# A hand-fused attention and gating kernel on one core: the same pieces of work in another order on every queue

## The chip, the core and the metric

The kernel runs on one core of one Trainium2 chip. A core has five instruction queues that run side by side: TensorE (PE, matmuls), VectorE (DVE), ScalarE (ACT), GpSimd (POOL) and SyncE (SP, which here only issues DMAs). Each takes its instructions strictly in the order in which they were written, and waits for what an instruction needs. The metric is the device time of one execution in microseconds; smaller is better.

## What is computed

Attention in which a query sees only the keys of its own cluster, for 4 batches, 8 heads, 768 positions and 64 features, and then a gated MLP on the joined heads:

```python
q_assign = np.argmax(np.einsum('bhsd,hcd->bhsc', q_n, c_n), axis=-1)   # 16 clusters a head
k_assign = np.argmax(np.einsum('bhsd,hcd->bhsc', k_n, c_n), axis=-1)
mask = q_assign[:, :, :, None] == k_assign[:, :, None, :]
scores = np.where(mask, scale * np.matmul(q, k.transpose(0, 1, 3, 2)), -1e9)
attn = np.exp(scores - np.max(scores, axis=-1, keepdims=True))
attn = attn / (np.sum(attn, axis=-1, keepdims=True) + 1e-09)
x = np.matmul(attn, v)                 # heads joined: 4 x 768 x 512
h = np.maximum(x @ w_in, 0.0)          # 512 -> 1024
u, v = h[..., :512], h[..., 512:]      # v is layer-normalised over its 512
v_s = np.einsum('ts,bsd->btd', w_spatial, v_n) + b_spatial[None, :, None]
out = (u * v_s) @ w_out                # 512 -> 512
```

## The kernel before

The work falls into pieces: a piece is a handful of instructions on one engine, or one DMA issue. The functions `prep`, `shifts`, `attend` and `mlp` (with `v_tile`, `u_tile`, `s_tile`, `p_tile`) only describe them to a plan: which engine, which pieces must be over first, which buffers are taken. The loop at L1156 goes through 4 batches of 4 pairs of heads and describes the preparation of the next pair, the attention of this pair, and after each batch its MLP. `Plan.run` then writes the program. What stands where on each queue is not decided by a rule: it is read from a table, one list of numbers for each engine, in which a number is the count of a piece among those of its engine:

```python
            own = [o for o in self.ops if o.eng == e]
            queue[e] = [own[int(k)] for k in ORDER.get(e, "").split()][::-1]
```

There are 847 pieces on PE, 730 on ACT, 967 on DVE, 294 on POOL and 330 on SP. Pieces of attention, of the preparation of later heads and of the MLP of the batch before stand mixed on each queue, so that PE has other work while a score waits for its exponential.

The pieces that come up below, by their lines:

- Head of the program: 76 filler matmuls on a constant tile (L560) run before and between the first pieces of PE; L586 transposes the centroids.
- Preparation of a pair: L695 casts the features to their high half (ACT), L704 makes the low half, L710 copies it (DVE), L741 to L743 are the cluster logits (PE), L760 to L764 the argmax on DVE, L772 and L773 the one-hot form (ACT), L788 brings its rows in beside the features and L789 copies features on (lo<-hq), both as DMAs that SP issues. L815 and L816 sum the values, L826 and L828 write their means. L859 (PE) and L866 (DVE) find row maxima of the scores, L878 to L882 turn them into shifts.
- Attention in row form, for the heads that a list names: scores L920 and L922 (PE), maximum and scale L925 to L927 (DVE), exponential L928 and its high half L930 (ACT), low half L931 (POOL), a DMA that transposes both (L936, p<-pt, issued by SP), values L940 (PE).
- Attention in column form, for the others: scores L956 and L958 (PE), exponential L962 and high half L964 (ACT), low half L965 (POOL), values L970 (PE). No DMA stands between.
- The attention's output is divided and split in L989 to L994 and transposed in L996.
- MLP: L1015 (matmuls for v and for the output), L1037 to L1049 the layer norm on DVE, L1050 (ACT) and L1051 (POOL) its halves vn, L1075 (matmuls for u and for the spatial mix), L1108 to L1113 the gate, L1138 and L1139 the output.

The buffers on which pieces wait for one another: 2 score buffers (sc) and 4 accumulators (acc) in PSUM; 6 tiles each of p in 32 bits (p32) and of its halves (pt); 3 of hq and lo; 2 of v32, 4 of u32.

Of the kernel before, what the change touches and what calls it, by code (L numbers as in the profile page):

```python
# [137 lines left out]
8 20 40 72 18 27 46 62 11 9 59 35 6 16 14 5 76 4 34 54 37 33 7 78 57 31 81 49 41 63 51 12 84 80 79 24 60 19 29 83 73 36 0 85 87 38 17 91 92 93 82 90 88 3 42 58 86 22 89 39 106 48 101 95 77  # L138
32 94 47 1 25 103 100 107 26 99 52 56 98 126 50 96 128 10 102 130 132 150 2 97 134 116 108 136 104 127 105 129 109 138 140 110 131 113 142 111 114 117 144 115 133 123 112 146 118 148 119 125
135 121 137 120 139 141 124 70 143 64 65 122 194 152 170 155 172 158 145 147 174 160 176 161 178 154 156 159 180 21 167 168 149 66 157 13 169 171 163 45 153 173 182 53 162 55 184 166 71 75  # L140
186 67 188 175 165 177 190 179 181 192 183 15 164 185 74 214 196 216 238 198 187 218 151 189 191 193 220 222 202 23 205 224 204 68 69 203 199 200 226 201 228 197 215 230 213 211 232 217 212
234 219 221 206 195 223 209 236 208 227 207 229 225 210 258 231 240 260 249 262 248 264 243 247 241 336 266 245 233 253 235 268 254 252 237 270 244 246 242 255 251 272 250 274 256 259 261 30
257 276 278 263 280 239 271 265 267 269 347 349 371 338 351 273 275 43 353 28 277 340 344 279 281 44 61 339 345 355 357 348 343 350 341 352 359 361 337 363 342 346 354 365 373 380 379 356
378 367 374 358 360 369 282 362 364 283 375 382 376 384 381 284 377 386 388 406 366 285 390 392 372 368 394 370 396 286 287 288 289 398 383 294 385 387 400 407 389 295 391 408 402 412 393
292 404 414 293 290 291 441 299 300 304 415 305 413 416 309 411 417 310 419 395 397 409 399 410 421 443 444 423 446 451 401 425 296 449 450 297 427 445 403 298 429 405 306 431 311 307 433
308 312 418 435 313 420 422 424 301 302 437 439 303 426 322 323 447 452 428 448 430 324 454 432 325 456 434 458 530 436 460 453 438 462 455 464 440 326 466 457 314 315 468 316 470 459 442
317 472 474 461 463 320 318 321 319 541 465 543 532 467 538 537 535 469 545 547 533 471 565 549 473 536 551 540 553 475 327 555 534 328 542 544 539 546 557 329 548 559 550 330 561 331 563
476 477 478 552 479 554 531 590 566 568 556 558 570 572 560 332 574 562 480 564 576 578 481 580 333 567 582 482 483 569 584 334 335 586 588 484 571 573 579 575 591 581 577 486 593 485 595
615 488 487 597 583 489 585 599 493 601 587 498 494 589 603 499 592 605 594 503 607 596 609 504 598 611 490 600 613 491 616 602 604 492 500 606 618 620 501 502 495 622 608 496 610 624 612
614 626 505 497 628 630 617 506 619 507 632 694 621 634 623 516 625 636 517 638 627 521 522 695 697 518 629 519 631 699 520 523 701 633 635 719 524 703 637 525 705 639 707 510 696 709 508  # L150
698 509 700 711 511 713 702 640 715 641 717 704 642 706 512 643 720 722 652 708 644 653 724 710 645 712 726 744 714 728 646 647 730 716 718 513 732 514 734 515 721 648 723 649 736 725 657
738 658 727 740 650 742 729 731 651 733 745 662 663 747 667 735 749 668 526 751 737 739 527 741 753 743 755 654 655 757 759 659 746 656 748 761 660 750 763 661 765 752 664 767 754 528 756
769 665 758 760 771 666 529 773 762 775 669 764 766 777 670 779 680 781 770 768 681 783 671 785 772 774 685 787 789 776 686 778 791 682 683 780 687 688 689 782 784 786 684 674 788 790 675
792 672 676 673 677 678 679 793 794 795 796 797 798 799 805 800 803 801 806 804 802 810 815 690 691 816 692 811 693 820 821 817 822 818 812 813 823 807 808 809 814 824 819 833 838 834 839
835 836 840 827 837 829 841 842 825 826 828 830 831 832 845 843 844 846
""",
    "ACT": """
0 1 23 24 2 35 36 25 28 27 26 29 31 30 32 44 46 45 47 7 50 33 51 34 38 40 37 39 8 48 49 85 86 59 61 60 63 65 62 64 41 43 42 67 66 69 68 72 88 87 74 70 73 76 78 75 77 53 54 55 80 123 124 52
# [1053 lines left out]
```

## Time and profile before

| | us |
|---|---|
| runs of the kernel before, median of 3 (lowest, highest) | 615.07 (614.6, 615.17) |
| profiled execution, its own time | 616.04 |
| its span in the trace | 614.2 |
| PE busy | 595.4 (97%) |
| DVE busy | 459.0 (75%) |
| ACT busy | 455.6 (74%) |
| POOL busy | 422.5 (69%) |

Busy time is time in which an engine works on an instruction; the rest of the span it waits or has nothing left to do. The granted clock of TensorE was 1.00 in the whole span. An engine's share is a mean over stages with different limits, so the rows further below are taken by stretch, and idle time is read with the engine that ended it.

### The profile page before, as it was taken

What the parts mean: (1) busy time and instruction counts of PE and PEld (TensorE: products, weight loads), DVE (VectorE), ACT (ScalarE), POOL (GpSimd) and SP (SyncE); (2) the same over time, 40 slices, a digit from 0 to 9 for tenths busy, and PEclk for the clock granted to TensorE, in tenths of its full rate; (3) what the DMA queues carried; (4) which work ended last, traced back from release to release, by engine and by line L of the source; (5) the groups of instructions that cost most, each with busy time, mean ns of one, the idle gap of its engine ahead of it and who ended that gap; (6) DMA issues with size and microseconds to landing.
All of it is one profiled execution on the core that took longest, in us unless ns stands there. A gap on an engine that the chain in (4) does not pass through costs nothing.

```text
span 614.2 us, 16911 instructions
## 1 busy us (share of the span) xinstructions
PE 595.4 (97%) x6779; PEld 378.4 (62%) x6779; DVE 459.0 (75%) x992; ACT 455.6 (74%) x706; POOL 422.5 (69%) x305
## 2 busy tenths in 40 slices
PE   8999999999999999999999999999989999999997
PEld 4566666666555576686565658855555668544573
DVE  6999999989998997689878788878865664242220
ACT  6789999998878688879878978778777886133012
POOL 2387998898776779697878776966877788133111
PEclk9999999999999999999999999999999999999999
DMA  6666664875489696969799999999999999600002
GB/s 218 153 163 143 194 152 101 183 186 149 127 158 178 180 192 161 187 156 194 184 201 177 192 191 214 193 195 219 197 196 202 166 198 183 128 17 35 18 1 102
DMA packets 224940, 98.05 MB, mean 160 GB/s; under 512 B 210647, under 2 KB 212510, under 8 KB 224862
## 3 DMA queue, kind: packets, MB, share of 16 engines
q1 hardware_dynamic: 221118, 90.48, 74.6%
q10 hardware_dynamic: 3744, 6.49, 3.1%
q8 instruction: 53, 0.87, 0.6%
q14 instruction: 25, 0.20, 0.1%
HBM read 27.63 MB, written 6.29 MB: 55 GB/s over the span
## 4 chain that ended last, share of the span: by engine, by line
PE 48%; DVE 6%; ACT 3%; DMA 2%; issue 2%; SPq 1%; POOL 0%; ACTq 0%; DVEq 0%; POOLq 0%
PE acc L1075 17%; PE acc L1015 15%; PE acc L940 6%; PE sc L920 4%; PE sc L922 4%; DVE rs L925 2%; ACT p L928 2%; PE acc L970 1%; DMA p<-pt 1%; DVE hq L710 1%; ACT pt L930 1%; DVE v L1049 1%; DMA lo<-hq 1%; SPq L936 0%; DVE vhl L798 0%
## 5 line engine op out<-in xcount | busy, mean ns | idle before, releaser
L931 POOL TENSOR_TENSOR pt<-p,pt 128x768 f16<-128x768 f32 x102 | 169.2, 1667 | 52.8 <-ACT pt L930 30.9
L965 POOL TENSOR_TENSOR pt<-p,pt 128x768 f16<-128x768 f32 x90 | 151.3, 1702 | 27.7 <-ACT pt L964 16.2
L925 DVE TENSOR_REDUCE rs<-sc 128x1 f32<-128x768 f32 x102 | 96.9, 952 | 47.8 <-PE sc L922 38.7
L928 ACT ACTIVATE p<-sc,rs 128x768 f32<-128x768 f32 x102 | 100.4, 990 | 41.6 <-DVE rs L927 24.0
L1075 PE MATMUL acc<-wsp,vn 128*128 128x512 f16 (+1 forms) x576 | 101.1, 326 | 0.0
L866 DVE TENSOR_REDUCE nm<-acc 128x1 f32<-128x512 f32 (+1 forms) x135 | 87.0, 682 | 8.4 <-PE acc L859 7.9
L930 ACT CAST pt<-p 128x768 f16<-128x768 f32 x102 | 83.4, 830 | 3.2 <-PE acc L970 2.1
L962 ACT ACTIVATE p<-sc 128x768 f32<-128x768 f32 x90 | 71.6, 810 | 6.3 <-PE sc L958 4.5
L1075 PEld LDWEIGHTS <-vn 128*128 128x128 f16 x576 | 54.9, 97 | 34.3
L940 PEld LDWEIGHTS <-p 128*128 128x128 f16 x1836 | 66.8, 97 | 14.4 <-DMA p<-pt 2.0
L964 ACT CAST pt<-p 128x768 f16<-128x768 f32 x90 | 72.7, 836 | 0.3
L940 PE MATMUL acc<-vhl,p 128*128 128x65 f16 (+1 forms) x1836 | 70.1, 193 | 0.4 <-DMA p<-pt 0.2
L1075 PE MATMUL acc<-xT,win 128*128 128x256 f16 (+1 forms) x384 | 68.4, 326 | 0.0
L1015 PE MATMUL acc<-win,xT 128*128 128x512 f16 x288 | 67.1, 379 | 0.0
L1015 PE MATMUL acc<-wou,ghl 128*128 128x512 f16 x264 | 61.6, 379 | 0.7 <-DVE xn L991 0.7
L970 PEld LDWEIGHTS <-pt 128*128 128x128 f16 x1620 | 57.1, 97 | 8.0 <-issue 0.6
L970 PE MATMUL acc<-vhl,pt 128*128 128x65 f16 (+1 forms) x1620 | 61.0, 193 | 0.1
L920 PE MATMUL sc<-lo,hq 128*128 128x512 f16 x204 | 49.8, 326 | 4.3 <-DMA lo<-hq 1.6
L1113 POOL TENSOR_TENSOR ghl<-u,ghl 128x512 f16<-128x512 f32 x22 | 26.3, 1199 | 37.3 <-ACT ghl L1112 33.0
L1075 PEld LDWEIGHTS <-win 128*128 128x128 f16 x384 | 36.4, 97 | 22.2
L922 PE MATMUL sc<-hq 80*128 80x512 f16 x204 | 50.0, 326 | 0.0
L859 PE MATMUL acc<-hq 80*128 80x512 f16 (+1 forms) x180 | 47.0, 325 | 2.3 <-DVE nm L866 2.3
(136 smaller groups left out, 962.2 us busy)
## 6 DMA issues: line engine op xcount, KB each, us to landing
raw<-in_kqT_dram SPq DMA_DIRECT2D x15, 768.0 KB
vraw<-in_vp_dram SPq DMA_DIRECT2D x16, 384.0 KB
out_dram<-wraw ACTq DMA_DIRECT2D x24, 256.0 KB
hq<-lo SPq DMA_DIRECT2D x16, 192.0 KB
lo<-hq SPq DMA_DIRECT2D x16, 192.0 KB
hq<-hq SPq DMA_DIRECT2D x6, 384.0 KB
wraw<-in_wsT_dram SPq DMA_DIRECT2D x6, 384.0 KB
wraw<-in_w_in_dram SPq DMA_DIRECT2D x4, 512.0 KB
```

Source lines behind the costliest of these rows:

```text
L866: V.tensor_reduce(out=nm.t[:, t, k:k + 1] if n == 1 else nm.t[:, t:t + n, k], in_=src, axis=AX.X, op=ALU.max, negate=True)
L920: T.matmul(out=sc.t[:, cs], lhsT=hq.t[:, 2, h, ks], rhs=lo.t[:, h, cs], start=True, stop=False)
L922: T.matmul(out=sc.t[:, cs], lhsT=hq.t[0:R_SH, 1, h, ks], rhs=hq.t[0:R_SH, 0, h, cs], start=False, stop=True)
L925: o = op("DVE", 0.95, lambda sc=sc, rs=rs: V.tensor_reduce(out=rs.t[:, 0:1], in_=sc.t[:, 0:S], axis=AX.X, op=ALU.max, negate=True), after= ...
L928: o = op("ACT", 0.99, lambda sc=sc, p32=p32, rs=rs: A.activation(out=p32.t, in_=sc.t[:, 0:S], func=AF.Exp, bias=rs.t[:, 2:3], scale=rs.t[: ...
L930: o = op("ACT", 0.83, lambda pt=pt, p32=p32: A.copy(out=pt.t[:, 0, :], in_=p32.t), after=[o], use=[p32], new=[pt], key=K_HI)
L931: o = op("POOL", 1.65, lambda pt=pt, p32=p32: G_.tensor_tensor(out=pt.t[:, 1, :], in0=p32.t, in1=pt.t[:, 0, :], op=ALU.subtract), after=[o ...
L940: T.matmul(out=av.t[:, k * (D + 1):k * (D + 1) + w], lhsT=rt()[:, c, :], rhs=rhs, skip_group_check=True, **f)
L965: o = op("POOL", 1.65, lambda pt=pt, p32=p32: G_.tensor_tensor(out=pt.t[:, 1, :], in0=p32.t, in1=pt.t[:, 0, :], op=ALU.subtract), after=[o ...
L970: T.matmul(out=av.t[:, t * (D + 1):t * (D + 1) + w], lhsT=lhsT, rhs=rhs, skip_group_check=True, **f)
L1015: T.matmul(out=acc.t, lhsT=lr[m][0], rhs=lr[m][1], start=(m == 0), stop=(m == n - 1))
L1075: T.matmul(out=o.rearrange("p (t q) -> p t q", q=P), lhsT=lr[m][0], rhs=lr[m][1], start=(m == 0), stop=(m == total - 1), skip_group_check= ...
```

## The change

Only the table changes. Each of its five lists holds the same numbers in another sequence. Nothing else of the program differs: the pieces, their instructions, their buffers and what each needs are the same. A line or two of each kind show the form (the first line of PE, and of ACT):

```diff
 ORDER = {
     "PE": """
-8 20 40 72 18 27 46 62 11 9 59 35 6 16 14 5 76 4 34 54 37 33 7 78 57 31 81 49 41 63 51 12 84 80 79 24 60 19 29 83 73 36 0 85 87 38 17 91 92 93 82 90 88 3 42 58 86 22 89 39 106 48 101 95 77
+59 18 57 17 16 7 20 37 73 62 35 11 29 34 5 54 40 76 8 31 46 27 9 72 4 6 33 78 81 56 51 12 14 49 48 84 80 79 10 41 19 60 36 38 83 0 42 85 90 1 58 39 92 88 24 87 86 93 22 47 63 89 52 82 91 106
...
     "ACT": """
-0 1 23 24 2 35 36 25 28 27 26 29 31 30 32 44 46 45 47 7 50 33 51 34 38 40 37 39 8 48 49 85 86 59 61 60 63 65 62 64 41 43 42 67 66 69 68 72 88 87 74 70 73 76 78 75 77 53 54 55 80 123 124 52
+0 1 23 24 2 35 36 26 27 28 25 30 32 29 31 44 46 45 7 47 37 33 34 50 38 51 40 39 49 48 8 85 86 59 61 60 63 65 62 67 41 43 42 64 66 68 69 70 72 87 88 74 76 73 78 52 75 77 53 55 54 80 123 124
...
```

On PE 323 of the 847 pieces keep their place in the list, on ACT 290 of 730, on DVE 385 of 967, on POOL 178 of 294 and on SP 133 of 330; 131 pieces of PE move by more than two places. Among the numbers of PE's first lines are those of the fillers L560: 22 of their matmuls stand ahead of the first L741 before, 26 after (16 and 17 of them ahead of L586).

Three places show what such a move is in the program. Names are those of the tiles, with the number of the buffer or of its use; `x2` counts equal instructions in a row.

ACT, where the profile of before stands at 118 to 123 us. `p32` are exponentials in 32 bits, `pt` their high halves, `sc0` and `sc1` the two score buffers. Before:

```order
L619 ACTIVATE win_104<-acc0_112 128x512
L964 CAST pt_2383<-p32_2231 128x768
L964 CAST pt_2391<-p32_2245 128x768
L964 CAST pt_2431<-p32_2276 128x768
L962 ACTIVATE p32_2437<-sc1_111 128x768
L879 ACTIVATE shx0_84<-nl_2433 128x6
L882 ACTIVATE shx0_84<-nl_2433 128x6
L964 CAST pt_2450<-p32_2306 128x768
L882 ACTIVATE shx0_84<-nl_2433 128x6
L962 ACTIVATE p32_2473<-sc0_110 128x768
```

After:

```order
L619 ACTIVATE win_104<-acc3_115 128x512
L964 CAST pt_2383<-p32_2224 128x768
L962 ACTIVATE p32_2404<-sc1_111 128x768
L964 CAST pt_2445<-p32_2260 128x768
L826 ACTIVATE wl0_93<-w32_2333 2x2x64
L964 CAST pt_2456<-p32_2275 128x768
L879 ACTIVATE shx0_84<-nl_2447 128x6
L882 ACTIVATE shx0_84<-nl_2447 128x6
L962 ACTIVATE p32_2471<-sc0_110 128x768
L882 ACTIVATE shx0_84<-nl_2447 128x6
L962 ACTIVATE p32_2497<-sc1_111 128x768
```

The exponential that empties `sc1` moved from behind three casts to behind one, and the next one, of `sc0`, ahead of a fourth cast.

SP, where the profile of before stands at 440 to 451 us: transposes of p for the values (L936), row copies of the one-hot form (L788) and the copy of a pair's features (L789, `lo<-hq`). Before:

```order
L788 DMA hq_7049<-oht_7804 16x768
L936 DMA_TRANSPOSE p32_7966<-pt_8005 128x12x128
L936 DMA_TRANSPOSE p32_7989<-pt_8059 128x12x128
L788 DMA hq_7049<-oht_7804 16x768
L936 DMA_TRANSPOSE p32_8088<-pt_8097 128x12x128
L788 DMA hq_7049<-oht_7804 32x768
L789 DMA lo_7183<-hq_7049 64x1536
L788 DMA hq_7049<-oht_7804 32x768
L936 DMA_TRANSPOSE p32_8104<-pt_8141 128x12x128
```

After:

```order
L788 DMA hq_7069<-oht_7747 32x768
L788 DMA hq_7069<-oht_7747 16x768
L936 DMA_TRANSPOSE p32_7790<-pt_7811 128x12x128
L936 DMA_TRANSPOSE p32_7907<-pt_7921 128x12x128
L692 DMA vraw_8025<-in_vp_dram 128x768
L788 DMA hq_7069<-oht_7747 32x768
L936 DMA_TRANSPOSE p32_7954<-pt_8004 128x12x128
L936 DMA_TRANSPOSE p32_7999<-pt_8011 128x12x128
L789 DMA lo_7184<-hq_7069 64x1536
L788 DMA hq_7069<-oht_7747 16x768
L936 DMA_TRANSPOSE p32_8076<-pt_8080 128x12x128
```

L789 stands ahead of a transpose that it stood behind (`p32_8088` before is `p32_8076` after), and the two row copies L788 that stood just ahead of it now stand further up; a load of values (L692) has come in between.

DVE, where the profile of before stands at 289 to 296 us: the end of a layer norm (L1045 to L1049, `y` is the inverse deviation of two tiles, `v32` the tiles) beside the argmax of another pair (L761 to L763). Before:

```order
L1045 SCALAR_TENSOR_TENSOR y2_5466<-y_5407 128x2
L710 COPY hq_5258<-hq_5258 64x1536
L1046 TENSOR_TENSOR y2_5466<-y2_5466,a_5402 128x2
L1047 SCALAR_TENSOR_TENSOR y_5407<-y2_5466,y_5407 128x2
L761 TENSOR_TENSOR acc0_112<-acc0_112,mx_5435 128x384
L1049 TENSOR_SCALAR v32_5345<-v32_5345,mv_5350,y_5407 128x512
L1049 TENSOR_SCALAR v32_5288<-v32_5288,mv_5350,y_5407 128x512
L989 TENSOR_SCALAR rc_5581<-acc1_113 128x6
```

After:

```order
L1045 SCALAR_TENSOR_TENSOR y2_5481<-y_5436 128x2
L1046 TENSOR_TENSOR y2_5481<-y2_5481,a_5431 128x2
L761 TENSOR_TENSOR acc1_113<-acc1_113,mx_5434 128x384
L1047 SCALAR_TENSOR_TENSOR y_5436<-y2_5481,y_5436 128x2
L1049 TENSOR_SCALAR v32_5290<-v32_5290,mv_5370,y_5436 128x512
L762 TENSOR_TENSOR acc1_113<-acc1_113,wt_78 128x384
L763 TENSOR_REDUCE m2_5550<-acc1_113 128x24
L1049 TENSOR_SCALAR v32_5328<-v32_5328,mv_5370,y_5436 128x512
```

The tile that was written first (the lower number, `v32_5288` before, `v32_5290` after) is now normalised first, and the argmax pieces stand between. Its cast on ACT (L1050) stands just ahead of the exponential for which PE waits at 296.92.

## Rows read from the trace of the kernel before

**Rows 1.** The page's busy table: us (share of the span), instructions.

```profile
PE 595.4 (97%) x6779; PEld 378.4 (62%) x6779; DVE 459.0 (75%) x992; ACT 455.6 (74%) x706; POOL 422.5 (69%) x305
```

**Rows 2.** Stretches: length, busy PE, PEld, DVE, ACT, POOL (instructions), PE clock, DMA, GB/s.

```profile
9.50:120.00 110.50, 104.41 (x1480) 71.11 (x1478) 108.79 (x210) 100.49 (x178) 85.08 (x55) 1.00 0.66 158
120.00:140.00 20.00, 18.43 (x304) 13.03 (x303) 17.46 (x36) 18.94 (x36) 20.00 (x14) 1.00 0.82 197
160.00:300.00 140.00, 137.38 (x1637) 88.97 (x1636) 121.94 (x247) 113.41 (x178) 107.07 (x75) 1.00 0.86 177
```

**Rows 3.** Timeline of PE's head: start, us, instruction, count, [idle before <- who ended it].

```profile
7.45 1.47 PE L560 MATMUL acc<-ones 128*128 128x512 f16 x6
8.76 0.18 PE L741 MATMUL acc<-cmh,hq 128*128 128x32 f16 x1
```

**Rows 4.** Timeline of DVE, the first L760 and 121 to 138.

```profile
9.49 0.36 DVE L760 TENSOR_REDUCE mx<-acc 128x12 f32<-128x192 f32 x1 [0.38 <-PE acc L743]
...
121.17 0.56 DVE L760 TENSOR_REDUCE mx<-acc 128x24 f32<-128x384 f32 x1 [0.31 <-PE acc L743]
...
125.63 1.29 DVE L866 TENSOR_REDUCE nm<-acc 128x2 f32<-128x512 f32 x2 [0.58 <-PE acc L859]
...
127.83 0.69 DVE L866 TENSOR_REDUCE nm<-acc 128x1 f32<-128x512 f32 x1 [0.91 <-PE acc L859]
...
134.78 0.69 DVE L866 TENSOR_REDUCE nm<-acc 128x1 f32<-128x512 f32 x1 [0.28 <-PE acc L859]
...
137.37 1.90 DVE L866 TENSOR_REDUCE nm<-acc 128x1 f32<-128x512 f32 x3 [0.30 <-PE acc L859]
```

**Rows 5.** Timeline of ACT, near 119 and near 296.

```profile
118.77 2.31 ACT L964 CAST pt<-p 128x768 f16<-128x768 f32 x3
120.96 0.84 ACT L962 ACTIVATE p<-sc 128x768 f32<-128x768 f32 x1
...
295.54 0.62 ACT L1050 CAST vn<-v 128x512 f16<-128x512 f32 x1 [2.31 <-DVE v L1049]
```

**Rows 6.** Timeline of PE, five waits and one use of a transpose.

```profile
121.84 0.48 PE L956 MATMUL sc<-hq,lo 128*128 128x512 f16 x2 [0.49 <-ACT p L962]
...
154.87 0.38 PE L816 MATMUL acc<-vs,one 128*2 128x128 f32 x2 [0.50 <-DVE vs L815]
...
188.90 0.38 PE L956 MATMUL sc<-hq,lo 128*128 128x512 f16 x1 [0.44 <-ACT p L928]
...
231.43 0.34 PE L940 MATMUL acc<-vhl,p 128*128 128x65 f16 x6
...
296.92 0.48 PE L920 MATMUL sc<-lo,hq 128*128 128x512 f16 x2 [1.18 <-ACT p L962]
...
453.62 0.50 PE L920 MATMUL sc<-lo,hq 128*128 128x512 f16 x2 [1.63 <-DMA lo<-hq]
```

**Rows 7.** Timeline of SP: a transpose's issue.

```profile
224.88 1.51 SPq L936 DMA_TRANSPOSE p<-pt  x1
```

**Rows 8.** Chain of waits: start, us, what.

```profile
446.50 1.46 SPq L936
...
448.93 4.65 DMA lo<-hq
...
486.98 6.08 DMA p<-pt
```

**Rows 9.** Timeline of DVE, near 292.

```profile
291.24 1.56 DVE L1047 SCALAR_TENSOR_TENSOR y<-y,y 128x2 f32<-128x2 f32 x1
...
293.20 2.31 DVE L1049 TENSOR_SCALAR v<-v,mv,y 128x512 f32<-128x512 f32 x2
```

**Rows 10.** Timeline of POOL, near 292.

```profile
291.15 1.64 POOL L965 TENSOR_TENSOR pt<-p,pt 128x768 f16<-128x768 f32 x1
293.36 1.86 POOL L965 TENSOR_TENSOR pt<-p,pt 128x768 f16<-128x768 f32 x1 [0.57 <-POOL pt L965]
```

**Rows 11.** L1047 over the whole span: shortest, median, longest in ns.

```profile
L1047 DVE SCALAR_TENSOR_TENSOR y<-y,y x12: 149/161/1565, 161.2 to 558.3; 128x2 f32<-128x2 f32 x12
```

128 rows, old and new, of the table ORDER are left out of this document.

## The prediction

> **What bounds the kernel now.** I read the busy table first: TensorE (PE) works 595.4 of 614.2 us [rows 1], at a granted clock of 1.00 in every stretch shown [rows 2], which is its upper level, 2.4 GHz. The order changes no instruction's kind or count, so PE's work stays, and all that an order can win lies in the 18.8 us in which PE stands still, or lose by adding to them. Part of that is head and tail. So next I read, on the timeline of PE, the starts with idle time before them, with the engine that ended it [rows 6], and followed each back on the engine named [rows 4, 5, 9, 10] or in the chain of waits [rows 8]. Two facts decide which places count. From 9.50 to 120.00 the vector engine (DVE) is busy 108.79 of 110.50 us while PE is busy 104.41 [rows 2]: here DVE sets the pace, and what DVE loses at its start is carried to the end of that stretch. From 160.00 on PE is busy 137.38 of 140.00 us [rows 2]: here each PE wait counts whole, and a wait of DVE or ScalarE (ACT) counts only where PE waits behind it.
>
> **The change part by part.** The plans of both kernels hold the same pieces, so I compare which piece stands ahead of which.
>
> (a) The head. Before, 22 of the filler matmuls (L560) stand ahead of the first logits (L741); after, 26. Six of them take from 7.45 to 8.76 [rows 3], where the clusters' matmul between them costs nothing that shows: 0.218 us each, so four cost 0.87. DVE's first L760 starts at 9.49 after an idle 0.38 for just these logits [rows 4]. The delay goes into the DVE-bound stretch, which has 110.50 − 108.79 = 1.71 us of slack in all, partly in front of waits that move with it. I take +0.8; ends 0 (slack takes it) and +0.87.
>
> (b) 121 to 138. DVE stands still five times for matmuls: 0.31, 0.58, 0.91, 0.28, 0.30, together 2.38 us [rows 4]. The row maxima that it waits for (L859 on PE, reduced in L866) stand on PE behind score matmuls L956, and the one at 121.84 waited 0.49 for ACT's exponential L962 [rows 6], which has to empty one of the two score buffers. ACT reaches that exponential at 120.96 only after three casts L964 that take 2.31 us [rows 5]. The new ACT order puts an exponential after the first of these casts, so two casts, 2.31 × 2/3 = 1.54 us, leave the way of the score buffers. The casts then come later, and GpSimd (POOL), busy 20.00 of 20.00 us here [rows 2], takes what they feed; that is what could eat the gain. Ends 0 and −2.38 (all five gone); I take −1.3, a little over half and under the 1.54, since only the first three waits are near that cast row.
>
> (c) Two PE waits, 0.50 at 154.87 for a DVE sum and 0.44 at 188.90 for a row-form exponential [rows 6]. In the new order 3.5 and 1.2 us of other PE work stand ahead of the waiting matmuls. The cover exceeds the waits, unless DVE and ACT are late by as much. −0.8; ends −0.94 and 0.
>
> (d) 453.62: PE waits 1.63 us for a DMA that copies the low parts of a head's features (lo<-hq, L789) [rows 6]. The chain shows why: the issuing queue (SP) spends 1.46 us on a transpose (446.50), then issues a row copy and at 448.93 the copy, which takes 4.65 us to land [rows 8]. The new order puts L789 ahead of that transpose and moves the two row copies just ahead of it further up, which brings it some 1.4 us earlier by the transpose alone, and PE has 0.8 us more of other work ahead of L920. 1.4 + 0.8 exceeds 1.63, so the wait goes. What is late next is the transpose that is issued behind it, by L789's own issue of about 0.8 us, for which (f) pays. −1.6; ends 0 and −1.63.
>
> (e) 296.92: PE waits 1.18 us for ACT's exponential L962 [rows 6]. ACT had started it at 296.07 behind L1050, which waited 2.31 us until 295.54 for DVE's L1049 [rows 5]. DVE did L1047 at 291.24 in 1.56 us, where its median is 0.161 [rows 9, 11], and then two L1049 in 2.31 us [rows 9], and the tile that ACT wants was the second. In the new order that tile comes first, and L761 goes ahead of L1047. If L1049 keeps its place in time, half of the pair, 1.15 us, is won; but L1047 at 291.24 ended with POOL's L965 (291.15 + 1.64 = 292.79), and the second L1049 ran beside POOL's next L965 (293.36 + 1.86 = 295.22) [rows 9, 10], so the small operations, or the first L1049, may again be stretched to POOL's end, and then only some 0.5 us is won. I take −0.9; ends −1.18 and 0.
>
> On these stretched operations there is a rule. The Trainium skill, *SBUF — State Buffer*, section "SBUF: two separate sides", says that DVE and GpSimd share a pair of ports under an exclusive lock, which the operation that starts first keeps for its whole length while the other is blocked. The trace agrees at 291.24, where a 0.161 us operation ended with POOL's at 292.79 [rows 9 to 11]. By that rule the L1049 put first waits out whatever POOL started before it, and (e) is −0.5 and the sum −2.2; by the pair's mean it is −1.15 and −2.9.
>
> (f) New waits. A p<-pt transpose (L936) takes from its issue to its use by the value matmuls L940; where PE actually waited for one it landed 6.08 us after its issue [rows 8], and one at 231.43 was used 6.55 us after its issue at 224.88 without a wait [rows 6, 7]. The new order takes 1.92 us of PE work from ahead of that use and puts a 0.72 us issue ahead of the transpose: 3.91 us are left. At six more of the 102 value pieces the distance falls by 1.2 us or more, to under 5.6 us. If such a transpose lands as that at 486.98 did, there is a wait of up to 2.2 us; if it lands in under 3.9 us, none. The landing of a transpose that nobody waited for isn't seen. I take +1.2, about one stretch of the five late in full; ends 0 and +6.6 (worked out in rival B).
>
> All other reorderings, by mostly under 3 us of their engine's work, I cost at 0: their covers are the two score buffers, four accumulators and six transposed tiles, and the waits that they carried are not among those read. If that cover is thin, (f) shows it. The tail stays in its length.
>
> Sum: +0.8 − 1.3 − 0.8 − 1.6 − 0.9 + 1.2 = −2.6 us. The profiled execution took 616.04 us, of which 614.2 are its span [rows 1]; it would take 613.4. The median of the runs, 615.07, lies 0.97 below it, and I put the change on the median: **612.5**.
>
> **The rivals.**
> A, the waits only move. POOL is busy for the whole of 120 to 140 [rows 2], so exponentials taken sooner meet a full set of six p tiles, which POOL empties at its own pace; then (b) is 0, and the pieces pulled ahead in (c) are waited for at the same time: 0. Left are +0.8 − 1.6 − 0.9 + 1.2 = −0.5: 614.6. For it speaks the POOL row; against it that POOL's 85.08 of 110.50 just before [rows 2] leaves tiles in hand.
> B, on the other side: transposes land after their use. Seven value pieces in five stretches (199, 229 to 233, 424, 449, 527) come within 3.9 to 5.5 us of their issue. At the 6.13 us that passed from 486.98 until the matmul that waited, the stretches fall short by 1.4, 2.2, 1.0, 0.6 and 1.4 us, each worked out as the one at 231.43: 6.6 in place of 1.2, a total of +2.8: 617.9. It decides from a landing of 5.8 us on (shortfalls 5.0, total +1.2). For it speaks that the one landing seen is 6.08 [rows 8]; against it that it is a landing somebody waited for, so the late end of a spread.
> C, more: (a) is swallowed by the slack, and (b) to (e) are won whole without (f): −2.38 − 0.94 − 1.63 − 1.18 = −6.1: 608.9. Against it: POOL in (b) and (e).
> That the change does nothing is a part of A, since the new order is what the queues really hold.
>
> **How the numbers follow.** Two measurements of this kernel that differ by under 0.2%, 1.23 us, can't be told from no change; same means that. The forecast's terms .50 (.44 faster, .06 same), A .20 (.17 same, .03 slower), B .16 slower, C .14 faster. So faster .58, same .23, slower .19. The range goes from 608.8, where C ends, up to 616.8, where B stands with a landing of 5.9 us; beyond it lie about .10 above and .08 below.
>
> **What would show it.** In the profile of the changed kernel: (a) DVE's first L760 at about 10.3 in place of 9.49. (b) L866 and L760 between 121 and 140 with less than 1.2 us of idle time together; if it stays over 2, A is right. (c) no idle time before L816 near 155 and the scores near 189. (d) no idle time over 0.3 before L920 near 453; if it is there, L789 landed later than 4.65 us after its issue. (e) the idle time before the scores near 297 under 0.4. (f) idle time of PE before L940, released by the DMA p<-pt, in the five stretches: in all about 1.2; over 5 is B. PE's busy time must stay within 0.5 of 595.4, and the granted clock at 1.00; if it falls, all of this sum is wrong. It is also wrong if PE's idle time grows at places not named here, by pieces that I cost at nothing.

## The result: slower by 0.5%, and the profile after

| | us |
|---|---|
| before, median of 5 runs (lowest, highest) | 614.77 (614.56, 615.17) |
| after, median of 5 runs (lowest, highest) | 618.31 (616.62, 619.12) |
| ratio after to before, 95% interval | 1.0053 (1.0037 to 1.007) |
| profiled execution after, its span | 619.12, 617.3 |

The forecast was 612.5, with a range up to 616.8; the kernel is 3.5 us slower instead. A second comparison of the same two kernels (e11 below) has 1.2 us, with an interval of 0.9998 to 1.0038, so that the size is known less well than the first interval says. PE's work is the same, so the loss is PE's idle time. The page's busy table of the changed kernel, against [rows 1]:

```profile
PE 594.7 (96%) x6779; PEld 378.5 (61%) x6779; DVE 459.0 (74%) x992; ACT 456.4 (74%) x706; POOL 423.9 (69%) x305
```

DVE's busy time is the same as before, 459.0. What changed is where it lies. The stretches of the changed kernel, with the columns of [rows 2]:

```profile
9.50:120.00 110.50, 103.33 (x1489) 71.22 (x1489) 108.23 (x210) 99.66 (x177) 85.99 (x56) 1.00 0.70 157
120.00:140.00 20.00, 17.93 (x300) 12.82 (x299) 18.02 (x35) 19.82 (x37) 19.25 (x13) 1.00 0.96 191
140.00:160.00 20.00, 16.70 (x204) 10.35 (x201) 19.77 (x25) 14.53 (x22) 14.23 (x9) 1.00 0.56 141
160.00:300.00 140.00, 137.99 (x1640) 88.97 (x1639) 120.76 (x251) 112.93 (x178) 105.15 (x72) 1.00 0.79 167
```

And the third of these stretches in the kernel before, which did not stand among the rows:

```profile
140.00:160.00 20.00, 19.48 (x230) 11.77 (x230) 19.68 (x35) 17.25 (x27) 16.45 (x10) 1.00 0.46 130
```

From 140 to 160 us PE does 2.78 us less than before (16.70 against 19.48), while DVE is as busy as before (19.77 against 19.68) with fewer instructions, 25 in place of 35. So DVE still sets the pace there, and some of its instructions take longer. The timeline says which. DVE of the changed kernel, all but the last rows of this part:

```profile
142.26 0.69 DVE L636 SCALAR_TENSOR_TENSOR acc<-wraw,acc 128x512 uint32<-128x512 uint32 x1
142.87 0.16 DVE L989 TENSOR_SCALAR rc<-acc 128x6 f32<-128x6 f32 x1
142.94 1.29 DVE L704 SCALAR_TENSOR_TENSOR lo<-raw,hq 128x768 f16<-128x768 f32 x1
144.15 2.40 DVE L798 SCALAR_TENSOR_TENSOR vhl<-vraw,vhl 128x768 f16<-128x768 f32 x1
...
147.23 0.68 DVE L620 SCALAR_TENSOR_TENSOR win<-acc,win 128x512 f16<-128x512 f32 x1
147.94 2.73 DVE L710 COPY hq<-hq 64x1536 f16<-64x1536 f16 x2
150.60 1.27 DVE L866 TENSOR_REDUCE nm<-acc 128x2 f32<-128x512 f32 x2
151.90 2.00 DVE L704 SCALAR_TENSOR_TENSOR lo<-raw,hq 128x768 f16<-128x768 f32 x1
153.83 1.27 DVE L866 TENSOR_REDUCE nm<-acc 128x2 f32<-128x512 f32 x2
155.02 2.15 DVE L620 SCALAR_TENSOR_TENSOR wsp<-wraw,wsp 128x768 f16<-128x768 f32 x1
```

POOL of the changed kernel beside it:

```profile
140.14 3.28 POOL L965 TENSOR_TENSOR pt<-p,pt 128x768 f16<-128x768 f32 x2
144.08 1.65 POOL L965 TENSOR_TENSOR pt<-p,pt 128x768 f16<-128x768 f32 x1 [0.67 <-ACT pt L964]
146.70 3.56 POOL L965 TENSOR_TENSOR pt<-p,pt 128x768 f16<-128x768 f32 x2 [0.96 <-ACT pt L964]
151.45 1.64 POOL L965 TENSOR_TENSOR pt<-p,pt 128x768 f16<-128x768 f32 x1 [1.20 <-ACT pt L964]
```

The same part of the kernel before, DVE:

```profile
141.76 0.70 DVE L636 SCALAR_TENSOR_TENSOR acc<-wraw,acc 128x512 uint32<-128x512 uint32 x1
142.36 1.07 DVE L798 SCALAR_TENSOR_TENSOR vhl<-vraw,vhl 128x768 f16<-128x768 f32 x1
143.36 0.95 DVE L704 SCALAR_TENSOR_TENSOR lo<-raw,hq 128x768 f16<-128x768 f32 x1
...
145.50 1.20 DVE L710 COPY hq<-hq 64x1536 f16<-64x1536 f16 x2
...
147.93 1.09 DVE L704 SCALAR_TENSOR_TENSOR lo<-raw,hq 128x768 f16<-128x768 f32 x1
...
150.53 2.41 DVE L620 SCALAR_TENSOR_TENSOR wsp<-wraw,wsp 128x768 f16<-128x768 f32 x1 [0.18 <-ACT wsp L619]
```

And its POOL:

```profile
140.98 1.64 POOL L965 TENSOR_TENSOR pt<-p,pt 128x768 f16<-128x768 f32 x1
143.92 1.89 POOL L965 TENSOR_TENSOR pt<-p,pt 128x768 f16<-128x768 f32 x1 [1.30 <-PE acc L970]
...
150.48 1.65 POOL L965 TENSOR_TENSOR pt<-p,pt 128x768 f16<-128x768 f32 x1
```

Read the starts in pairs. After, L798 starts at 144.15, 0.07 us behind POOL's L965 (144.08), and takes 2.40 us where it took 1.07; it ends 0.82 us after that L965 (146.55 against 145.73). Before, L704 starts at 143.36, ahead of POOL's L965 (143.92), takes its usual 0.95, and the L965 takes 1.89 in place of 1.65: whoever starts second waits. After, the two L710 take 2.73 in place of 1.20, and the second L704 2.00 in place of 1.09 (it starts at 151.90, L965 at 151.45). The operations on PSUM keep their time beside the same POOL operations: L620 of w_in takes 0.68 wholly inside an L965 (from 146.70 on), and two L866 take 1.27 although an L965 starts under the second of them (151.45). PE, on the same stretch of the changed kernel, waits for what stands behind the long ones:

```profile
147.37 0.38 PE L859 MATMUL acc<-hq 80*128 80x256 f16 x2 [1.52 <-DVE xn L991]
...
151.32 0.38 PE L859 MATMUL acc<-hq 80*128 80x512 f16 x1 [0.38 <-DVE nm L866]
...
154.56 0.18 PE L741 MATMUL acc<-cmh,hq 128*128 128x32 f16 x1 [0.95 <-DVE nm L866]
```

All waits of PE that this trace lists between 120 and 160 us end on DVE; none ends on POOL, so a low half that POOL finishes late is not what PE waits for.

This gave the theory. **L**: in a DVE-bound stretch the new order brings DVE operations with operands in SBUF to their start just behind POOL's L965, and they are held until it ends. The Trainium skill, *SBUF — State Buffer*, section "SBUF: two separate sides", has this as an exclusive lock on a shared pair of ports, for DVE operations in a two-port mode, or with two inputs in SBUF against a GpSimd operation that reads SBUF; whoever starts first keeps it for the whole instruction. The pairs of starts above agree, in both directions. The rivals: **O**, PE's row maxima stand behind too many other pieces, and the long durations are only a sign of it; **T**, transposes that land late; **M**, many small shifts; **S**, the sequence of DVE in this stretch as such.

### The profile page after: what moved, and what is told of

Its sections match the earlier page's. It is cut to its first block, busy times and chain, and to the rows that moved or that the text cites. A ratio compares the mean times of both kernels' runs of the same rounds, so it can differ in the third digit from the quotient of the medians.

```text
span 617.3 us, 16914 instructions
## 1 busy us (share of the span) xinstructions
PE 594.7 (96%) x6779; PEld 378.5 (61%) x6779; DVE 459.0 (74%) x992; ACT 456.4 (74%) x706; POOL 423.9 (69%) x305
## 4 chain that ended last, share of the span: by engine, by line
PE 60%; DVE 11%; ACT 5%; DMA 3%; issue 2%; POOL 1%; ACTq 0%; DVEq 0%; POOLq 0%
PE acc L1075 21%; PE acc L1015 17%; PE acc L940 7%; PE sc L920 5%; PE sc L922 4%; PE acc L970 3%; DMA p<-pt 3%; DVE rs L925 2%; ACT p L928 2%; DVE nm L866 1%; PE sc L956 1%; PE sc L958 1%; DVE hq L710 1%; DVE lo L704 1%; ACT p L962 1%
## 5 line engine op out<-in xcount | busy, mean ns | idle before, releaser
L965 POOL TENSOR_TENSOR pt<-p,pt 128x768 f16<-128x768 f32 x90 | 152.1, 1713 | 23.6 <-ACT pt L964 14.1
L866 DVE TENSOR_REDUCE nm<-acc 128x1 f32<-128x512 f32 (+1 forms) x135 | 86.8, 681 | 6.5 <-PE acc L859 6.0
L940 PEld LDWEIGHTS <-p 128*128 128x128 f16 x1836 | 67.3, 97 | 15.4 <-DMA p<-pt 2.5
L964 ACT CAST pt<-p 128x768 f16<-128x768 f32 x90 | 72.8, 833 | 0.3
L940 PE MATMUL acc<-vhl,p 128*128 128x65 f16 (+1 forms) x1836 | 70.4, 193 | 1.0 <-DMA p<-pt 0.8
L970 PEld LDWEIGHTS <-pt 128*128 128x128 f16 x1620 | 57.5, 97 | 8.0 <-issue 0.9
L970 PE MATMUL acc<-vhl,pt 128*128 128x65 f16 (+1 forms) x1620 | 61.2, 193 | 0.0
L859 PE MATMUL acc<-hq 80*128 80x512 f16 (+1 forms) x180 | 46.3, 325 | 5.8 <-DVE nm L866 3.0
L920 PE MATMUL sc<-lo,hq 128*128 128x512 f16 x204 | 49.7, 325 | 2.1 <-ACT p L928 1.8
L1108 DVE TENSOR_TENSOR acc<-acc,bbc 128x512 f32<-128x512 f32 x24 | 16.7, 694 | 42.3 <-PE acc L1075 42.2
```

Source lines behind the costliest of these rows:

```text
L866: V.tensor_reduce(out=nm.t[:, t, k:k + 1] if n == 1 else nm.t[:, t:t + n, k], in_=src, axis=AX.X, op=ALU.max, negate=True)
L920: T.matmul(out=sc.t[:, cs], lhsT=hq.t[:, 2, h, ks], rhs=lo.t[:, h, cs], start=True, stop=False)
L940: T.matmul(out=av.t[:, k * (D + 1):k * (D + 1) + w], lhsT=rt()[:, c, :], rhs=rhs, skip_group_check=True, **f)
L965: o = op("POOL", 1.65, lambda pt=pt, p32=p32: G_.tensor_tensor(out=pt.t[:, 1, :], in0=p32.t, in1=pt.t[:, 0, :], op=ALU.subtract), after=[o ...
L970: T.matmul(out=av.t[:, t * (D + 1):t * (D + 1) + w], lhsT=lhsT, rhs=rhs, skip_group_check=True, **f)
```

## The experiments

Each ratio is to runs of the kernel before on the same chip. The middle columns come from each kernel's profile. To see how much DVE time was lengthened I add up L798, the two L704, the pair of L710 and L620 of wsp between 141 and 157 us (in the changed kernel 2.40 + 1.29 + 2.00 + 2.73 + 2.15 = 10.57) and take off what they take where POOL does not meet them (0.95 + 2 x 0.95 + 1.03 + 0.95 = 4.83).

| kernel | lengthened, us | PE busy 140 to 160, us | median us | before, us | ratio (95%) |
|---|---|---|---|---|---|
| before | 1.89 | 19.48 | | | |
| changed | 5.74 | 16.70 | 618.31 | 614.77 | 1.0053 (1.0037 to 1.007) |
| e1 new order to 160 us | 4.85 | 17.74 | 617.94 | 615.05 | 1.0036 (1.0006 to 1.0065) |
| e2 new order from 160 us | 1.89 | 19.48 | 613.3 | 615.05 | 0.9951 (0.9924 to 0.9978) |
| e3 changed, POOL cut | 0.32 | 19.36 | 612.87 | 615.05 | 0.9965 (0.9942 to 0.9988) |
| e4 before, POOL cut | 0.13 | 20.00 | 613.93 | 615.05 | 0.9972 (0.9943 to 1.0001) |
| e5 changed, DVE reordered | 1.95 | 19.44 | 613.93 | 614.96 | 0.9977 (0.9964 to 0.9991) |
| e6 before, DVE 1.45 us late | 3.91 | 15.82 | 619.22 | 614.96 | 1.0065 (1.0045 to 1.0086) |
| e7 new order 266 to 300 | 1.88 | 19.48 | 613.54 | 614.96 | 0.9978 (0.996 to 0.9997) |
| e8 new order 105 to 141 | 4.37 | 16.82 | 618.04 | 614.96 | 1.0052 (1.0029 to 1.0074) |
| e9 two windows and L815 | 0.74 | 19.97 | 613.09 | 615.65 | 0.9966 (0.9941 to 0.9991) |
| e10 DVE's sequence alone | 1.75 | 19.45 | 615.58 | 615.65 | 0.9993 (0.9973 to 1.0013) |
| e11 changed, again | 3.49 | 18.27 | 616.87 | 615.65 | 1.0018 (0.9998 to 1.0038) |

The five kernels with over 3 us of lengthened time (changed, e1, e6, e8, e11) are the five slowest, and their PE works 15.82 to 18.27 us of these 20; the other eight have under 2 us and 19.36 to 20.00. The lengthened time is that of one traced execution each, and that execution can lie off its median: by 3.9 us above in e3 (616.76), by 2.6 below in e8 (615.47).

**Where: e1 and e2.** The two orders cut together at 160 us.

```diff
 each list of ORDER
-all pieces in the old sequence
+e1: pieces that started before 160 us in the profile of before: new sequence; the rest: old
+e2: pieces that started before 160 us: old sequence; the rest: new
```

> The new order for all pieces that started before 160 us in the profile of before, the old order for the rest. Theory L (the loss is made between 142 and 158, where DVE operations with operands in SBUF run into POOL's L965 and are held): this kernel takes the whole loss and none of the later gains, +3.7 to +4.3 us, 618.5 to 619.1. Rival T (the loss comes from transposes that land late after 160): within 1 us of before. Rival M (many small shifts over the whole kernel, each a tenth of a us): about half of the measured +3.5, so +1.5 to +2.

> The old order for all pieces that started before 160 us, the new order for the rest. Theory L: only the gains near 296 and 453 and the small waits around them are left, -1.0 to -1.6 us, 613.2 to 613.8. Rival T: +3 to +4. Rival M: +1.5 to +2.

e1 is 2.9 us slower than before, e2 1.75 us faster. The loss lies in the first 160 us, the gain behind it. T falls by both, M by e2 (e1's interval alone would allow it). e1 lies 0.6 us under the range written for it, e2 inside its own, and the intervals are 3 to 4 us wide; the two together make +1.2 us, which is what e11 (below) has and less than the first comparison's 3.5.

**What: e3 and e4.** POOL's share is taken away for six tiles, in either kernel; both leave out the low halves of these tiles.

```diff
-lambda pt=pt, p32=p32: G_.tensor_tensor(out=pt.t[:, 1, :], in0=p32.t, in1=pt.t[:, 0, :], op=ALU.subtract)
+lambda pt=pt, p32=p32, c=8 if 57 <= pt.n <= 62 else S: G_.tensor_tensor(out=pt.t[:, 1, 0:c], in0=p32.t[:, 0:c], in1=pt.t[:, 0, 0:c], op=ALU.subtract)
...
-mm(t, D + 1, pt.t[:, 1, ts], vh.t[:, k, h, 0:D + 1], start=False, stop=stop)
+mm(t, D + 1, pt.t[:, 0 if 57 <= pt.n <= 62 else 1, ts], vh.t[:, k, h, 0:D + 1], start=False, stop=stop)
```

> The changed kernel, in which the POOL operation L965 of six key tiles (those that run between 144 and 158 us) takes 8 columns in place of 768; their low halves are left out of the values, which read the high halves in their place, so the matmuls stay. Theory L: with POOL almost idle there, the DVE operations L798, L710, L704 and L620 between 143 and 158 fall back from 2.0 to 2.4 us to 0.55 to 1.1 us, and the kernel is 3.5 to 5 us faster than the changed one: 613.5 to 615. Rival O (the row maxima simply stand behind too many other pieces on DVE, and the long durations are only what a waiting engine shows): the durations stay or the loss stays, 617.5 to 618.5.

> The kernel before with the same six L965 cut to 8 columns (the same low halves left out). Theory L: its DVE has 1.8 us of lengthened operations in this stretch (L620 at 150.53 alone 1.45), of which 0.5 to 1.8 us come back: 613 to 614.3, so that this kernel and the changed one with the same cut differ by under 1 us. Rival O: the same time as before, and the cut pair differs by 3 us or more.

Rows of DVE in e3, and one of its six cut POOL operations; they lie some 4 us later than in the changed kernel, behind a stretch from 50 to 60 us in which this execution had a granted clock of 0.66 on TensorE:

```profile
148.18 0.98 DVE L798 SCALAR_TENSOR_TENSOR vhl<-vraw,vhl 128x768 f16<-128x768 f32 x1
...
150.55 1.03 DVE L710 COPY hq<-hq 64x1536 f16<-64x1536 f16 x2
...
152.81 0.96 DVE L704 SCALAR_TENSOR_TENSOR lo<-raw,hq 128x768 f16<-128x768 f32 x1
```

```profile
148.15 0.20 POOL L965 TENSOR_TENSOR pt<-p,pt 128x8 f16<-128x8 f32 x1 [0.71 <-ACT pt L964]
```

L798 again starts just behind an L965 (148.18 and 148.15), but that one is over after 0.20 us, and L798 takes 0.98 in place of 2.40. The sequence of all queues is the changed one, and the loss is gone: 612.87, 2.2 us faster than before and 1.1 us faster than the kernel before with the same cut. That is 0.6 us under the range written for it, and the pair differs by 1.1 us where under 1 was expected. O would have kept 3 us or more between the two. So the long durations are the loss and not a sign of it, and POOL's work is what makes them.

**Whether it is the moment: e6 and e10.** e6 adds harmless DVE work ahead of the stretch, e10 gives DVE alone the new sequence inside it.

```diff
 e6, kernel before, L866
-V.tensor_reduce(out=..., in_=src, axis=AX.X, op=ALU.max, negate=True)
+for _ in range(3 if acc.n == 240 else 1):
+    V.tensor_reduce(out=..., in_=src, axis=AX.X, op=ALU.max, negate=True)
```

```diff
 e10, kernel before, list of DVE, in names
-L798 vhl, L704 lo, L990, L620 win, L991 xn, ... L866 acc243, L866 acc247
+L704 lo, L798 vhl, L990, L991 xn, L620 win, ... L866 acc247, L866 acc243
```

> The kernel before, in which one row maximum on DVE (L866 at 140.37) is written three times, which adds 2 x 0.60 = 1.2 us of DVE work that no POOL operation can hold up. Theory L: the operations behind it come 1.2 us later against POOL's, so L704 meets L965 (143.92) in place of missing it: the kernel is slower by 2.4 us or more, 617.3 to 619, with 1.2 us or more of lengthened DVE time more than before. Rival O: by 1.2 us at the most, 615.5 to 616.2.

> The kernel before, in which DVE alone has between 142 and 151 us the sequence that the changed kernel has there: L704 ahead of L798, L991 ahead of L620 of w_in, and two row maxima exchanged. Theory L in its strict form (what counts is the moment at which the DVE operation meets POOL's, not the sequence): L704 from 142.4 waits 0.2 us for POOL's L965 that ends at 142.62, and L798 then starts near 143.3, ahead of POOL's next at 143.92, so no collision of over 0.5 us on these two: within 1 us of before, lengthened DVE time in the stretch under 3 us. Rival S (the sequence itself makes the loss): 2.5 to 4 us slower, 617.5 to 619, and 4 us or more of lengthened time.

DVE in e6, and POOL's operation that it met (the added line moves the number of L965 to L966):

```profile
143.91 0.95 DVE L798 SCALAR_TENSOR_TENSOR vhl<-vraw,vhl 128x768 f16<-128x768 f32 x1
144.78 2.40 DVE L704 SCALAR_TENSOR_TENSOR lo<-raw,hq 128x768 f16<-128x768 f32 x1
...
148.34 2.68 DVE L710 COPY hq<-hq 64x1536 f16<-64x1536 f16 x2
```

```profile
144.01 2.35 POOL L966 TENSOR_TENSOR pt<-p,pt 128x768 f16<-128x768 f32 x1 [1.31 <-ACT pt L965]
```

The two added row maxima took 1.45 us (three in 2.13, against 0.68 for one), not the 1.2 expected, and cost 4.3 us. L798 starts 0.10 us ahead of L966 and holds it (2.35), then L966 has the turn and holds L704 (2.40), and so on down to the next L704 (1.77 at 152.25). The sequence is the old one. In e10 the sequence is the new one and the moment the old:

```profile
142.45 1.07 DVE L704 SCALAR_TENSOR_TENSOR lo<-raw,hq 128x768 f16<-128x768 f32 x1
143.44 0.95 DVE L798 SCALAR_TENSOR_TENSOR vhl<-vraw,vhl 128x768 f16<-128x768 f32 x1
```

L798 starts at 143.44, half a us ahead of the next L965 (144.01), and keeps its 0.95 us, and the kernel takes the time of before (0.9993). S falls, and the moment is what counts.

**What moved the moment: e8.** The new order only where ACT's exponentials go ahead of the casts.

```diff
 each list of ORDER
-all pieces in the old sequence
+pieces that started between 105 and 141 us in the profile of before: new sequence; the rest: old
```

> The kernel before with the new order only for the pieces that started between 105 and 141 us, where ACT's exponentials go ahead of casts. The prediction's term (b): 1.3 us faster, 613.7. What the changed kernel's trace suggests (PE 0.5 us later at 142 than at 120): 0 to +0.6 by itself, 615 to 615.6; theory L adds that any shift of DVE against POOL at 142 can bring collisions behind it, so up to +3 more, with as much lengthened DVE time between 142 and 158.

DVE and POOL in e8:

```profile
142.71 2.40 DVE L704 SCALAR_TENSOR_TENSOR lo<-raw,hq 128x768 f16<-128x768 f32 x1
```

```profile
142.65 1.64 POOL L965 TENSOR_TENSOR pt<-p,pt 128x768 f16<-128x768 f32 x1 [0.68 <-ACT pt L964]
```

This part alone costs 3.1 us, by the same chain: L704 0.06 us behind L965. In the kernel before, the second of the two long DVE operations starts 0.56 us ahead of that L965 (143.36 and 143.92). Two changes together take this lead away. The POOL operation before it ends later against DVE (in the changed kernel at 143.42, 0.47 us after L636 is through at 142.95; before at 142.62, 0.16 us after 142.46), so the first long operation is held longer, and the second can start only 1.20 us after L636 ends in place of 0.90. And the L965 in question starts 1.13 us after L636 ends in place of 1.46. The 0.30 and the 0.33 us together exceed 0.56; neither does alone. These distances are those of the order and not of one execution: 1.10 to 1.13 us in the traces of the changed kernel, e1, e5, e8 and e11, and 1.46 to 1.48 in those of before, e2, e4, e7, e9 and e10. What releases that L965 is, as far as the times show, ACT's cast L964, in either kernel: the L965 starts 0.13 us after the cast ends (143.92 after 143.79, 144.08 after 143.95).

```profile
142.98 0.81 ACT L964 CAST pt<-p 128x768 f16<-128x768 f32 x1
```

```profile
143.14 0.81 ACT L964 CAST pt<-p 128x768 f16<-128x768 f32 x1
```

The first of these rows is of the kernel before, the second of the changed one. The row of POOL before names PE's L970, which ended at 143.84, 0.05 us after the cast. So between 105 and 141 us the new order moved the other queues against DVE's, just where the prediction hoped to win 1.3 us.

**Whether it can be mended: e5 and e9.** e5 moves DVE pieces of the changed kernel between 143 and 157 us, e9 puts the two useful windows into the kernel before and moves L815.

```diff
 e5, changed kernel, list of DVE, in names
-L989, L704, L798 vhl, L990, L991, L620 win, L710, L710, L866, L866, L704, L866, L866, L620 wsp
+L704, L989, L990, L991, L620 win, L710, L710, L866, L866, L704, L866, L866, L798 vhl, L620 wsp
```

```diff
 e9, kernel before
+pieces that started between 225 and 252 and between 266 and 300 us: new sequence
 list of DVE near 150, in names
-L866, L620 wsp, L760, L815 vs
+L866, L815 vs, L620 wsp, L760
```

> The changed kernel with 14 DVE pieces between 143 and 157 us in another sequence, nothing else touched: L798 goes from right behind the first L704 to behind the last row maximum, and the operations that read PSUM (L989, L990, L991, L620 of w_in) come to stand right behind that L704, where POOL's L965 runs. Theory L (DVE and POOL hold each other off, whoever starts first): the operations on PSUM run through beside POOL, L798 and the two L710 fall into POOL's pauses, lengthened DVE time in this stretch falls from 5.7 us to under 3, and the kernel is 2 to 4 us faster than the changed one, 614.3 to 616.3. Rival O (what counts is which PE pieces stand behind the row maxima): L866 comes no earlier by this than the 1.1 us that L798 takes by itself, so at most 1.1 us faster, 617.2 to 618.3.

> The kernel before with the new order only for the pieces that started between 225 and 252 and between 266 and 300 us, and with one DVE piece moved: the sum of the values L815 goes ahead of L620 of wsp at 150.53, an operation that POOL's L965 (started 150.48) lengthened by 1.45 us. Theory L: L815 runs through beside POOL, L620 comes at POOL's next change and is lengthened by under 1 us, and PE's wait of 0.50 for L815 at 154.87 goes; with 1.2 near 296 and up to 0.8 near 240 the kernel is 1.5 to 2.5 us faster than before, 612.5 to 613.5, faster than both kernels of the case. Rival O: nothing from the moved piece, 613.0 to 614.

e5 takes the changed kernel from 1.0053 of before (1.0018 in e11) to 0.9977, by 14 pieces of one queue, and its interval lies under both of the changed kernel's: the lengthened time falls from 5.74 (3.49 in e11) to 1.95 us. e9 has 613.09, 2.6 us faster than before on its chip; L620 of wsp takes 1.25 there in place of 2.41, and L815, a reduction of one operand in SBUF, took 1.52 beside POOL, against 1.49 in e4, where POOL's operations there take 0.2 us. Its interval overlaps those of e2, e5 and e7, so which of the four is best stays open; all four beat both kernels of the case.

**The other terms: e7 and e11.**

```diff
 each list of ORDER
-all pieces in the old sequence
+e7: pieces that started between 266 and 300 us in the profile of before: new sequence; the rest: old
```

> The kernel before with the new order only for the pieces that started between 266 and 300 us. If the term (e) of the prediction stands, the wait of PE near 296.92 (1.18 us, for the exponential behind the layer norm) goes and the kernel is 0.9 to 1.4 us faster, 613.6 to 614.1. If POOL's L965 holds the layer norm's operations in the new order too, it is within 0.4 us of before.

> The changed kernel once more, unchanged. Theory L: a second trace shows L798, L710 and L704 between 143 and 155 us lengthened again, 4 to 6 us in all, since nothing random stands between them and the head; 617 to 619. If these were chances of one execution, they lie elsewhere or are under 2.5 us in the second trace. The wait of 1.63 us near 453 (lo<-hq), which the profile of before had and four traces with the old order at that place had not, has to be absent as well.

e7 is 1.4 us faster than before. The waits of PE in e10, where the old order stands at that place, still have the one of [rows 6]; e7 reaches its L920 there (294.70) without one. The row of e10:

```profile
297.44 0.48 PE L920 MATMUL sc<-lo,hq 128*128 128x512 f16 x2 [1.16 <-ACT p L962]
```

e11's trace shows the same first collisions as the first trace of the changed kernel: L798 at 142.95 in 2.43 us behind an L965 at 142.92, and the L710 2.73. The last two operations of the chain, L704 and L620 of wsp, got through this time (0.96, 0.95), so the lengthened time is 3.49 us and not 5.74, and not the 4 to 6 expected. The rows of the first collision in e11, DVE and POOL:

```profile
142.95 2.43 DVE L798 SCALAR_TENSOR_TENSOR vhl<-vraw,vhl 128x768 f16<-128x768 f32 x1
```

```profile
142.92 1.65 POOL L965 TENSOR_TENSOR pt<-p,pt 128x768 f16<-128x768 f32 x1 [0.71 <-ACT pt L964]
```

The time is 616.87, 1.2 us over before, and its interval just touches 1. In the two traces the size of the loss varies, its place doesn't.

## Why the prediction was wrong

The step that failed is the sentence "All other reorderings ... I cost at 0: their covers are the two score buffers, four accumulators and six transposed tiles". These covers hold waits for data. What the new order changed between 142 and 157 us was not a wait for data but the time at which DVE and POOL touch SBUF together, and in a DVE-bound stretch nothing covers that: 5.74 us of lengthened DVE operations in place of 1.89, and 2.78 us less PE work between 140 and 160. With it failed the worst end of (b), which I had put at 0: the part of the order that (b) is about sets off the chain and costs 3.1 us by itself (e8). The sum, step by step:

| term | forecast, us | shown |
|---|---|---|
| (a) head | +0.8 | DVE's first L760 0.2 us later in the median of the traces, 0.52 in the first |
| (b) 121 to 138 | -1.3 | DVE some 0.8 us sooner at 142; e8, this part alone: +3.1 |
| (c) 154.87 and 188.90 | -0.8 | both waits gone; the first lies inside the loss |
| (d) 453.62 | -1.6 | 0: the wait was that of one execution |
| (e) 296.92 | -0.9 | e7: -1.4 |
| (f) new waits for transposes | +1.2 | 0.8 us in the first trace, 0.5 in e11; not clear of chance |

(a) The size was too large. DVE's first L760 in the changed kernel:

```profile
10.01 0.36 DVE L760 TENSOR_REDUCE mx<-acc 128x12 f32<-128x192 f32 x1 [0.64 <-PE acc L743]
```

That is 0.52 us after the one of [rows 4]. But in this execution PE also stood still for 0.88 us before L586, which it did for 0.22 in e11. Over all traces L760 starts at 9.39 to 10.01 with the new head (median of five 9.41) and at 9.11 to 9.49 with the old one (median of eight 9.21). Nor is it the head that brings the collisions: in e11 L636 is through at 141.80, 0.66 us sooner than in the trace of before, and in e8 the head is the old one. Besides, PE stands still for 5.6 to 5.9 us between 20 and 120 in the traces of the changed kernel, e1, e5 and e11, and for 4.1 to 5.4 in the eight with the old order there. That is some 0.8 us more, in the stretch in which DVE sets the pace; no run separates the head from the other reorderings in it.

(b) was right about the waits and wrong about what they are worth. DVE's idle time for L859 and L743 between 118 and 142 us fell from 2.4 to 1.6 us, less than forecast. DVE used it: from its first L760 until L636 is through, 132.5 us pass in the median of five traces with the new order between 105 and 141 (132.3 to 132.9), and 133.3 in that of six with the old (132.4 to 133.7). It gained nothing by that, since it came to the next stretch at another moment against POOL. The part on (b) named POOL as what could eat the gain, as an engine that is full. It did so in another way, by holding DVE back. Rival A (614.6) stopped at a lost gain.

(d) was a misreading of one execution. The profiled execution of before took 616.04 us, 0.97 over the median, and I took that difference off the whole sum. But 1.63 us of it is this very wait [rows 6]. In the traces of e1, e4, e6, e7, e8, e9 and e10, which all have the old order there, PE does not wait for lo<-hq at all. So an order could win it only in an execution that has it, and the median of before is no such one. The other traces have such waits too: PE waited 2.0 us for a transpose (p<-pt) near 195 us in e4 and near 200 in e6, and not in the trace of before, whose order is the same there. When a profiled execution lies a whole microsecond over its median, a long DMA wait in it is the first suspect.

(e) was right, and its size within what e7 can tell (-2.5 to -0.2): the tile that ACT needs first is normalised first. POOL holds the small operations in the new order too, as the prediction feared, but the wait goes all the same. DVE in e7:

```profile
290.55 1.26 DVE L1047 SCALAR_TENSOR_TENSOR y<-y,y 128x2 f32<-128x2 f32 x1
291.85 1.10 DVE L1049 TENSOR_SCALAR v<-v,mv,y 128x512 f32<-128x512 f32 x1
```

L1047 ends with POOL's L965 again (290.15 + 1.64 = 291.79), and the one L1049 that ACT needs is through 2.4 us after L1047 began, where before the pair was through 4.3 us after it.

(f) is open. PE waited 0.8 us in all for p<-pt, against 0.2 before, so rival B, which made 6.6 us of it, did not come. But only one of the two waits, 0.52 at 201.56, lies at a place that (f) named, the other is at 516, and the 2.0 us of e4 and e6 near 200 came with the old order. The landing of 6.08 us in [rows 8] on which (f) and B rest was also hardly waited for: PE's work before that L940 ended 0.08 us before it.

No rival named the mechanism, though its rows were in hand: [rows 9 to 11] show a 0.161 us operation held for 1.56 us by an L965, and the prediction used them for one place only, at 296. The question to ask there was where else DVE operations on SBUF stand beside L965, in a stretch where DVE sets the pace. L620 of wsp at 150.53 with 2.41 us stood in the trace of before, 0.05 us behind an L965 (150.48), and DVE was busy 19.68 of the 20 us from 140 to 160: such a stretch. I had ended the DVE-bound stretch at 120.

Open is how much of the loss a given execution takes (3.5 and 1.2 us in two comparisons), and whether the two windows of e9 or L815 make its gain. Part of the first goes with TensorE's clock. In the comparison of e11, the changed kernel's executions with a mean granted clock of 0.999 or 1.00 (3 of 10) took 617.3 us in the median and those with 0.996 or 0.997 took 616.16; in the kernel before, the same two groups took 615.09 (21 of 28) and 618.07. So at full clock the loss there is 2.2 us, and a lower clock is not what makes it. Why the changed kernel has the lower clock more often (10 of its 15 executions in both comparisons), and whether that let the last two operations through in e11's trace (mean 0.997), isn't shown.

## What to carry to other kernels

When a change only moves instructions, look for stretches in which DVE is busy without a gap, list in them the DVE operations that work on SBUF next to long POOL operations on SBUF, and see who starts first and by how much: here a DVE operation that started 0.03 to 0.07 us behind POOL's took over 1.4 us more, and one such meeting brought the next. Put DVE operations on PSUM where POOL runs and those on SBUF in POOL's pauses, as e5 did. And before a wait for a DMA is counted as a gain, see whether the profiled execution lies above its median, since such a wait can be that execution's alone; a second profile of the same kernel tells.

## What the runs showed of the hardware

That a POOL operation holds a DVE operation was known from one row; that it holds it for its whole length (2.40 us for L798 or L704 that started 0.06 to 0.07 us behind a POOL operation of 1.65), and that 1.45 us of DVE work can cost 4.3 us by it (e6), was not. Not all DVE work is held: reductions and products on PSUM kept their 0.55 to 0.69 us, and L815, which reduces one operand in SBUF, took 1.52 beside POOL in e9 and 1.49 in e4.

The granted clock of TensorE can fall in the lossy stretch: in e1 and e11 its mean was 0.91 from 140 to 160 us, between its upper level (1.00, 2.4 GHz) and its lower (1.2 GHz), where PE had waited 1.52 us at 146.43 and 1.51 at 146.20; in the first trace of the changed kernel it stayed at 1.00 after a wait of the same length at 147.37. The row of e1:

```profile
140.00:160.00 20.00, 17.74 (x203) 10.72 (x202) 19.76 (x26) 15.18 (x22) 13.28 (x9) 0.91 0.50 132
```

What a fall costs there is not shown: it went with 3 us more in the executions of the kernel before (618.07 against 615.09), and with 1.1 less in those of the changed one (616.16 against 617.3).
